# The branch of slot 2 ahead of positions and rounding: a hand-over from attention to experts

## The chip, the cores and the metric

One core of one Trainium2 chip runs the whole program in one launch. The metric is device time in microseconds (us), from the start of the program to its end. The engines are TensorE (PE in the profile; its weight loads are PEld), VectorE (DVE), ScalarE (ACT), GpSimd (POOL) and SyncE (SP, which issues most DMAs). Each engine works through a queue of its own in program order and waits on semaphores of the others.

## The reference

Three layers follow one another on 4608 tokens (batch 8, sequence 576) of 512 features:

```python
k_p, v_p = k.reshape(B, H, 72, 8, D).mean(3), v.reshape(B, H, 72, 8, D).mean(3)   # pooled by 8
attn = softmax(q @ k_p.T / sqrt(64));  x = attn @ v_p            # 8 heads of 64
e_idx = argmax(x @ w_gate);  gate_w = softmax(x @ w_gate)[e_idx]  # 8 experts, one for each token
eom = sigmoid(x @ w_output_gate)
for e in range(8):                                               # w1 (512, 1024), w2 (1024, 512)
    out[e_idx == e] = gate_w * eom[:, e] * (relu(x[e_idx == e] @ w1[e]) @ w2[e])
g = s * relu(out @ w_in) ** 2 + b                                # w_in (512, 2048)
result = g @ w_out                                               # w_out (2048, 512)
```

## The kernel before

Products that need more than the engine's fast format gives are made from a high and a low part: ScalarE writes the high part, another engine subtracts it from the raw value to get the low part (`split`), and TensorE adds three products, high by high, high by low, low by high. So a "cut" of a tile is one ScalarE and one VectorE instruction.

**Attention** goes over 36 tiles of 128 tokens (`NT` = 36), as a pipeline written out by hand: iteration t transposes q of tile t+1 (`s1`), makes the scores of tile t (`s2`: matmuls, then VectorE's maximum L279 and subtraction L282), multiplies the weights of tile t-3 by v (`s4`, L329), transposes the weights of tile t-2 (`s3`, L307), and finishes tile t-4 on VectorE (`s5`, L341 to L357; L357 writes x, which SyncE stores to DRAM at L360). Scores and results have a PSUM tile each (`sc`, `pv`), used in turn. `fill` puts small steps of the router between VectorE's own. At the end of an iteration come its `hooks`: loads of expert 0's weights w1 and w2 and their cutting into eight pieces each (`wt.piece`): ScalarE makes the high part (L1042), another engine the low part (L1044). For w1 the low part is VectorE's, one piece in every second iteration from 20 on; for w2 it is GpSimd's, one in each iteration from 29 on.

**The router** (`Router`) gives each token a place in the list sorted by expert. It counts with matmuls against a triangle (L698 to L705), then writes for each tile a row matrix (`row`, L816), compares tile offsets with slot numbers (`compare`, L856), and inverts the list with 40 small matmuls (`invert`, L864), so that `idx` (L870) holds for each slot of 128 places the tokens to be gathered. It is done in two parts, columns `PRE` to `SOON` (2 to 5) first and the rest later. `tables` (L896 to L923) writes for each slot whether the expert changes (`chg`) and which comes next (`nxt`). `close_ranks` (L926 to L970) corrects the positions for the slots that were done ahead and writes `st`, where each slot's result is stored.

**Slots 0 and 1** belong to expert 0 and are filled from the first 16 tiles, so that TensorE has work while the router finishes (`First`): gather, transpose (`turn`), cut, layer one (L541, 24 matmuls for a slot), relu (L549), transposed h (`turn_h`, L555), its high and low part (`high_h`, `low_h` L565; they lie in the memory of the two slots' x). `Router.finish` runs router steps with this between them.

**`experts`** takes the slots one after another: layer one of slot i (`l1`, L1238 to L1240, 24 matmuls), layer two of slot i-1 (`l2`, L1268, 24 matmuls, PSUM tile `py`, two in turn), transposed h of slot i (`trh`, L1252), transposed x of slot i+2 (`tr`, L1228, PSUM tile `pt`, two in turn). `sw1` and `sw2` are the switches of the weights: ScalarE, VectorE and SyncE load `chg` into a register and branch (L1058, L1059); if the expert changes they cut the loaded weights. `later` holds work that is put behind the next slot's layer one: the cut of x and `result` (L1216, a copy out of PSUM by ScalarE and VectorE, and a store). `side(i, part)` runs a step of `Doubles`, which rounds the last layer's weights from 64-bit words (L1139 to L1156; VectorE, GpSimd and ScalarE in turn), and in slot 3 `token_scale`.

The order ahead of slot 2 is: `l2` of slot 0, `side(0, 0)` with `close_ranks`, `side(0, 1)`, `tr(2)`, `trh` of slot 1, `tr(3)`, `cut_h`, `side(1, 0)`, `side(1, 1)`, `sw1(2)`, layer one of slot 2.

**`Dense`** does the last two layers from about 690 us on.

Of the kernel before, what the change touches and what calls it, by code (L numbers as in the profile page):

```python
# [9 lines left out]
F32 = mybir.dt.float32  # L10
# [39 lines left out]
def attention(ctx, tc, c, q, k, v, wg, wog, xd, lg, ro, wt, room, hooks):  # L50
# [9 lines left out]
    spare = wt.pool.tile([P, 8192], F32, tag="wb", name="kvr")  # L60
    krs = [t[0:KB, 0:kv].rearrange("p (j f) -> p j f", j=NBLK) for t in (spare, wt.raw[1][0])]
    vrs = [spare[:, kv * i:kv * i + kv].rearrange("p (j f) -> p j f", j=NBLK) for i in (1, 2)]
    xbuf = [one.tile([P, DM], F32, name=f"x{i}") for i in range(3)] + [room]
    xbuf = [t.rearrange("p (a h d) -> p a h d", a=2, h=4) for t in xbuf]
    kbd = [one.tile([P, H, 2, SP], F32, name=f"kbd{i}") for i in range(3)]
    vbd = [one.tile([P, NSEG, VW], F32, name=f"vbd{i}") for i in range(3)]
# [271 lines left out]
    def s5(t, pv):  # L338
        pvv = pv[:, :, 0:4 * VW].rearrange("p a (h w) -> p a h w", w=VW)
        rec = p2.tile([P, 2, 4], F32, tag="rec", name="rec")  # L340
        nc.vector.tensor_scalar(out=rec, in0=pvv[:, :, :, VW - 1], scalar1=1e-9, scalar2=None, op0=ALU.add)  # L341
        fill()
        nc.vector.reciprocal(out=rec, in_=rec)
        fill()
        lp = p2.tile([P, 2, 4, G2], F32, tag="lp", name="lp")
        nc.vector.tensor_tensor(
            out=lp, in0=pvv[:, :, :, D:D + G2], in1=rec.unsqueeze(3).to_broadcast([P, 2, 4, G2]), op=ALU.mult
        )
        fill()
        nc.vector.tensor_reduce(  # L350
            out=lg[:, t, :], in_=lp.rearrange("p a h g -> p g (a h)"), axis=AX.X, op=ALU.add
        )
        fill()

        def rest():
            x = xbuf[t % 4]
            nc.vector.tensor_tensor(  # L357
                out=x, in0=pvv[:, :, :, 0:D], in1=rec.unsqueeze(3).to_broadcast([P, 2, 4, D]), op=ALU.mult
            )
            nc.sync.dma_start(out=xd[t * P:(t + 1) * P, :], in_=x.rearrange("p a h d -> p (a h d)"))  # L360

        if t == NT - 1:
            return rest
        rest()
# [58 lines left out]
    for t in range(NT + 4):  # L423
        if t < NT - 5:
            load_q(t + 5)
        if t < NT - 1:
            s1(t + 1)
        rest = s5(*pvs.pop()) if pvs else None
        mask_g()
        if t < NT:  # L430
            s2(t)
        for fn, a in sched.get(t, []):
            fn(*a)
        if t in (NT, NT + 1):
            s3(t - 2)
        if t == 28:
            first.gather(xd)
        if t == NT + 2:
            first.open()
            first.turn(0, ps.tile([P, 512], F32, tag="pe", name="pt0"))  # L440
            first.turn(1, ps.tile([P, 512], F32, tag="pf", name="pt1"))
        if 3 <= t < NT + 3:
            s4(t - 3)
        if 2 <= t < NT:
            s3(t - 2)
        if exps:
            exp_(*exps.pop())
        if t >= NT - 1:
            fill(5)
        while later:  # L450
            later.pop()()
        for a, b in BATCHES:
            if b == t - 3:
                fill(0 if b == NT else 99)
                todo += ro.steps(a, b, lambda: ps.tile([P, 512], F32, tag="prep", name="pr"), later)
        for fn in at_end.get(t, []) + hooks.get(t, []):
            fn()
        if t == NT + 2:
            first.cut(0)
    left, last = todo[:-5], todo[-5:]  # L460
    for f in last:
        f()
        if left:
            left.pop(0)()
    first.layer(0, ps.tile([P, 2, 512], F32, tag="pv", name="ph0"))
    first.run(12)
    first.relu(0)
    first.run(8)
    psv = later.pop()()
    first.run(4)  # L470
    rest()
    first.cut(1)
    for f in left:
        f()

    def between():
        first.relu(1)
        first.layer(1, ps.tile([P, 2, 512], F32, tag="sc", name="ph1"))
        first.run(8)
        first.turn_h(ps.tile([P, 2, 512], F32, tag="pv", name="th0"))  # L480
        first.run(4)
        first.relu(0)

    def behind():
        first.high_h()
        first.run(12)
        first.relu(1)

    inv = [ps.tile([P, NSLOT], F32, tag=n, name="inv") for n in ("pq", "pe")]
    ro.finish(psv, inv, between, behind, first.low_h)  # L490
    return first


class First:
# [35 lines left out]
    def layer(self, i, ph):  # L530
# [2 lines left out]
        wh, wl = [w.rearrange("p (k f) -> p k f", f=FE) for w in self.wt.a]  # L533
        for n in range(2):
            s = slice(n * 512, n * 512 + 512)
            o = ph[:, n]
            for k in range(4):
                for x, w in ((xh, wh), (xh, wl), (xl, wh)):
                    self.todo.append(
# [6 lines left out]
            self.todo.pop(0)()  # L546

    def relu(self, n):
        self.nc.scalar.activation(out=self.hs[self.i][n], in_=self.ph[:, n], func=AF.Relu)  # L549

    def turn_h(self, th):
        self.th = th
# [57 lines left out]
NSLOT = NT + E - 1 + PRE  # L610
ROOM = 5120
WIDE = 4
SOON = 5
MID = N - 2048
BATCHES = [(0, 8), (8, 16), (16, 24), (24, 30), (30, 34), (34, 36)]

# [1 line left out]
class Router:  # L618
# [204 lines left out]
    def finish(self, psv, inv, between, behind, last):  # L823
# [48 lines left out]
            )  # L872


        compare(0, NT, PRE, SOON)
        for step in rows:
            step()
        between()
        invert(inv[0], PRE, SOON)
        for t in range(0, 24, 8):  # L880
            compare(t, t + 8, SOON, NSLOT)
        index(inv[0], PRE, SOON)
        behind()
        compare(24, 32, SOON, NSLOT)
        compare(32, NT, SOON, NSLOT)
        invert(inv[1], SOON, NSLOT)
        last()
        index(inv[1], SOON, NSLOT)
        self.tables()
        V.scalar_tensor_tensor(  # L890
            out=kp["pos"], in0=self.ki, scalar=float(P), in1=self.rf, op0=ALU.mult, op1=ALU.add
# [294 lines left out]
            self.nc.gpsimd.tensor_tensor(out=b[:, o], in0=b[:, x], in1=b[:, y], op=op)  # L1186


def experts(ctx, tc, c, kp, wt, xd, ys, bank, wide, side, ahead, tail, start):
    nc = tc.nc  # L1190
    ident = c["ident"]
    p1 = ctx.enter_context(tc.tile_pool(name="ex1", bufs=1))
# [64 lines left out]
        for n in range(2):  # L1257
            split(nc, hh[n], hl[n], th[n])

    def l2(py, end=False, hh=hh, hl=hl):  # L1260
        wh, wl = [w.rearrange("p (k f) -> p k f", f=DM) for w in wt.b]
        ah, al = [[h[k // 4][:, k % 4 * P:k % 4 * P + P] for k in range(8)] for h in (hh, hl)]
        steps = [[(ah[k], wh[:, k]), (ah[k], wl[:, k]), (al[k], wh[:, k])] for k in range(8)]
# [1 line left out]
            steps = [[s[0] for s in steps], [s[1] for s in steps], [s[2] for s in steps]]  # L1265
        steps = [s for part in steps for s in part]
        for j, (a, w) in enumerate(steps):
            nc.tensor.matmul(py, lhsT=a, rhs=w, start=j == 0, stop=j == len(steps) - 1)  # L1268
        return py

# [21 lines left out]

    gather(2)
    gather(3)
    py = l2(room_y(), True, start.hh, start.hl)
    second(1)
    side(0, 0)
    side(0, 1)
    tr(2)()
    gather(4)  # L1300
    th = trh(start.hs[1])
    wt.raw_new(0)
    second(0)
    later = [tr(3)]
    gather(5)
    cut_h(th)
    later.append(lambda: result(0, py))
    side(1, 0)
    side(1, 1)
    sw1(2)  # L1310
    total = None

    def first(i):
# [7 lines left out]

    def slot(i):
        first(i)
        py = l2(room_y())
        th = trh()
        if i + 2 < NSLOT:
            later.append(tr(i + 2))
        side(i, 0)
        gather(i + 4)
        cut_h(th)  # L1330
# [375 lines left out]
def kernel(  # L1706
# [50 lines left out]
        hooks.setdefault(25 + j, []).append(lambda j=j: wt.load(1, slice(0, 1), part=j))  # L1757
    for j in range(8):
        for what in range(2):
            hooks.setdefault(20 + 2 * j + what, []).append(lambda j=j, w=what: wt.piece(0, j, 8, w))  # L1760
            hooks.setdefault(29 + j + what, []).append(lambda j=j, w=what: wt.piece(1, j, 8, w, nc.gpsimd))
    hooks[29].insert(0, wt.open_b)
    with ExitStack() as x:
        ro = Router(tc, c, lg, kp, wf)
        start = attention(x, tc, c, q, k, v, moe_w_gate, moe_w_output_gate, xd, lg, ro, wt, wf[:, ROOM:ROOM + DM], hooks)
# [13 lines left out]
    def side(i, part):  # L1779
        ahead(i, part)  # L1780
        if part == 0:
            if i == 0:
                close_ranks(tc, c, wide(), kp)
            db.step()
        else:
            if i == 3:
                token_scale(tc, wide(), lg, kp, tok.scale)
            if i % 3 != 2:
                db.step()
            if i > 3:  # L1790
                tok.order(kp["pos"], 1 + (i % 4 == 0))
# [17 lines left out]
    with ExitStack() as x:  # L1809
# [19 lines left out]
            dn.due(8)  # L1829
            db.run(db.end, len(db.pieces))  # L1830

        experts(x, tc, c, kp, wt, xd, ys, bank, wide, side, ahead, tail, start)
    dn.run(ctx)


# [24 lines left out]
```

## Time and profile before

| | |
|---|---|
| median of three runs | 1456.26 us (1454.87 to 1456.47) |
| the profiled execution's own time | 1453.35 us |
| its span, first to last instruction | 1451.5 us |
| TensorE busy | 1405.8 us (97%) |
| VectorE, ScalarE, GpSimd busy | 829.8, 710.3, 438.5 us |
| mean granted TensorE clock | 0.994 of 2.4 GHz |
| chain that ended last: TensorE | 43% of the span |

Busy time is the union of the instructions of an engine; matmuls are pipelined and their ends are modelled. The granted clock is the share of 2.4 GHz that TensorE was given, 0.50 being 1.2 GHz. Idle time is put down to the engine whose semaphore came last.

### The profile page before, as it was taken

The page shows a single profiled execution, that of the slowest core. Times are in us where ns is not written, and L with a number is a line of the kernel's source. Part 1 is how long each engine was busy: PE and PEld are TensorE (multiplying, and loading weights), DVE is VectorE, ACT ScalarE, POOL GpSimd, SP SyncE. Part 2 cuts the span into 40 slices and gives each one's busy share as a digit, 9 for nine tenths or more (in the row PEclk, how much of TensorE's full clock was granted, in tenths as well). Part 3 has the DMA queues.
Part 4 walks back from the last instruction along what each step waited for, and adds up shares of the span by engine and source line. Part 5 has one row for each costly group of instructions (what it writes and reads, how often), then busy time and mean ns, then how long its engine had stood idle before and what let it go on. Part 6 is the DMA issues. An engine that isn't in the chain of part 4 may idle for free.

```text
span 1451.5 us, 22908 instructions
## 1 busy us (share of the span) xinstructions
PE 1405.8 (97%) x7565; PEld 1235.3 (85%) x7565; DVE 829.8 (57%) x1680; ACT 710.3 (49%) x1324; POOL 438.5 (30%) x587
## 2 busy tenths in 40 slices
PE   5999987999999999999999999999999999999998
PEld 5898876888888888888898888898888889888887
DVE  6788874587845668423666544644553464455433
ACT  3666632365634455222656545545555554555443
POOL 4998333454565558307330100010010001001001
PEclk9999998999999999999999999999999999999999
DMA  9996234278775767594765654475465447545441
GB/s 252 298 313 191 95 108 163 88 207 222 209 216 182 217 181 260 151 85 123 244 160 138 181 139 129 118 192 142 116 182 141 126 122 192 139 116 160 118 117 64
DMA packets 203040, 239.43 MB, mean 165 GB/s; under 512 B 66702, under 2 KB 114062, under 8 KB 202894
## 3 DMA queue, kind: packets, MB, share of 16 engines
q1 hardware_dynamic: 195502, 217.22, 54.1%
q0 software_dynamic: 7392, 20.49, 4.9%
q8 instruction: 63, 1.03, 0.3%
q14 instruction: 83, 0.68, 0.2%
HBM read 184.39 MB, written 43.83 MB: 157 GB/s over the span
## 4 chain that ended last, share of the span: by engine, by line
PE 43%; issue 8%; ACT 1%; POOL 0%; DVE 0%; DMA 0%; POOLq 0%; DVEq 0%; ACTq 0%
PE po L1651 8%; PE po L1650 8%; PE po L1649 7%; PE bank L1590 7%; PE bank L1591 7%; PE bank L1592 7%; PE py L1268 0%; POOL out L1661 0%; DMA ring<-ws 0%; ACT wb L1614 0%; ACT y L1613 0%; ACT r L1613 0%; POOLq L1856 0%; ACT yo L1660 0%; ACT hs L1613 0%
## 5 line engine op out<-in xcount | busy, mean ns | idle before, releaser
L1613 ACT ACTIVATE r<-r,s_b 128x384 f32<-128x384 f32 x188 | 133.4, 710 | 275.5 <-DVE r L1606 247.9
L1661 POOL DMA_INDIRECT out<-yo,kp_pos x36 | 35.8, 993 | 662.9 <-ACT yo L1660 537.3
L1268 PE MATMUL py<-wb,hh 128*128 128x512 f32 x608 | 186.3, 389 | 0.3 <-ACT hh L994 0.3
L1605 DVE TENSOR_TENSOR r<-bank,held 128x384 f32<-128x384 f32 x141 | 78.4, 556 | 183.2 <-PE bank L1592 181.7
L1590 PE MATMUL bank<-wa,ring 128*128 128x384 f32 x480 | 162.2, 338 | 1.1 <-ACT xg L1596 0.9
L1591 PE MATMUL bank<-wa,ring 128*128 128x384 f32 x480 | 162.1, 338 | 0.0
L1592 PE MATMUL bank<-wa,ring 128*128 128x384 f32 x480 | 161.0, 335 | 0.0
L1650 PE MATMUL po<-wo,wb 128*128 128x512 f32 x396 | 156.5, 395 | 0.0
L1616 DVE TENSOR_TENSOR wb<-r,wb 128x384 fp32r<-128x384 f32 x188 | 104.7, 557 | 67.7 <-ACT wb L1614 67.7
L1651 PE MATMUL po<-wo,wb 128*128 128x512 f32 x360 | 143.0, 397 | 0.0
L1649 PE MATMUL po<-wo,wb 128*128 128x512 f32 x360 | 140.0, 389 | 0.0
L1268 PEld LDWEIGHTS py<-wb,hh 128*128 128x128 f32 x608 | 114.0, 188 | 24.1 <-ACT hh L994 0.5
L1238 PE MATMUL bank<-wa,xh 128*128 128x512 f32 x296 | 119.7, 404 | 11.6 <-ACTq L1059 11.6
L1141 POOL TENSOR_SCALAR dt<-dt 128x256 f32<-128x256 f32 x64 | 71.4, 1116 | 178.7 <-DVE dt L1140 170.3
L994 ACT ACTIVATE hh<-th 128x512 fp32r<-128x512 f32 x76 | 41.4, 595 | 170.7 <-PE th L1252 170.6
L1268 PE MATMUL py<-wb,hl 128*128 128x512 f32 x304 | 117.4, 390 | 0.0
L1240 PE MATMUL bank<-wa,xl 128*128 128x512 f32 x296 | 116.3, 393 | 0.0
L1239 PE MATMUL bank<-wa,xh 128*128 128x512 f32 x296 | 115.9, 391 | 0.0
L1590 PEld LDWEIGHTS bank<-wa,ring 128*128 128x128 f32 x480 | 90.1, 188 | 16.0 <-ACT r L1602 4.7
L1614 ACT ACTIVATE wb<-r 128x384 fp32r<-128x384 f32 x188 | 98.9, 526 | 6.0
L1591 PEld LDWEIGHTS bank<-wa,ring 128*128 128x128 f32 x480 | 90.1, 188 | 10.4
L995 DVE TENSOR_TENSOR hl<-th,hh 128x512 fp32r<-128x512 f32 x76 | 48.9, 683 | 82.6 <-ACT hh L994 82.6
(305 smaller groups left out, 3195.7 us busy)
## 6 DMA issues: line engine op xcount, KB each, us to landing
ring<-ws SPq DMA_DIRECT2D x336, 256.0 KB
wr<-in_moe_w SPq DMA_DIRECT2D x72, 512.0 KB
ws<-wf SPq DMA_DIRECT2D x16, 896.0 KB
ys<-y SPq DMA_DIRECT2D x37, 256.0 KB
q<-in_q SPq DMA_DIRECT2D x16, 512.0 KB
kvr<-in_v SPq DMA_DIRECT2D x8, 1024.0 KB
dx<-in_moe_w_out SPq DMA_DIRECT2D x32, 256.0 KB
dx<-in_moe_w_in SPq DMA_DIRECT2D x32, 256.0 KB
```

The source lines that it names most:

```text
L1238: nc.tensor.matmul(ph, lhsT=xh[:, k], rhs=wh[:, k, s], start=k == 0, stop=False)
L1239: nc.tensor.matmul(ph, lhsT=xh[:, k], rhs=wl[:, k, s], start=False, stop=False)
L1240: nc.tensor.matmul(ph, lhsT=xl[:, k], rhs=wh[:, k, s], start=False, stop=k == 3)
L1268: nc.tensor.matmul(py, lhsT=a, rhs=w, start=j == 0, stop=j == len(steps) - 1)
L1590: nc.tensor.matmul(o, lhsT=w[:, 0, k], rhs=xh[:, k], start=f, stop=False, skip_group_check=True)
L1591: nc.tensor.matmul(o, lhsT=w[:, 0, k], rhs=xl[:, k], start=False, stop=False, skip_group_check=True)
L1592: nc.tensor.matmul(o, lhsT=w[:, 1, k], rhs=xh[:, k], start=False, stop=False, skip_group_check=True)
L1613: lambda: nc.scalar.activation(out=r, in_=r, func=AF.Identity, scale=s_b[:, 0:1], bias=s_b[:, 1:2]),
L1616: [lambda: nc.vector.tensor_tensor(out=gl, in0=r, in1=gh.bitcast(F32), op=ALU.subtract)],
L1649: nc.tensor.matmul(o, lhsT=gh[:, s], rhs=wh, start=first, stop=False)
L1650: nc.tensor.matmul(o, lhsT=gh[:, s], rhs=wl, start=False, stop=False)
L1651: nc.tensor.matmul(o, lhsT=gl[:, s], rhs=wh, start=False, stop=last)
```

## The change

- In `experts`, `tr(2)` is issued in the middle of slot 0's second layer (after 12 of its 24 matmuls), and `sw1(2)` stands right behind the loads of the next weights. `close_ranks` and the router's second part (inversion and index of the later slots, now `others`, with a PSUM tile of `pt`) come in slot 2, behind its layer one. The four rounding steps of slots 0 and 1 go; slots 2, 5, 8 and 11 have one more each. The result of slot 0 (`y0`) is queued in slot 2, so that it runs in slot 3.
- `SOON` is 6 instead of 5: the first part of the index serves the gathers up to slot 5.
- In `Router.finish` the first index comes before slot 1's first layer has gone on, `low_h` before the last two compares.
- w2's low parts are made on VectorE. w1's pieces are cut one in each iteration from 19 on, w2's from 28 on.
- x has a fifth buffer for tiles below 24, in the memory of k and v.
- Slot 0's x is transposed and cut one iteration earlier, slot 1's one step earlier; the PSUM tiles that `First` uses are others.

```diff
-    xbuf = [one.tile([P, DM], F32, name=f"x{i}") for i in range(3)] + [room]
+    xbuf = [...] + [room, spare[:, 3 * kv:3 * kv + DM]]
-            x = xbuf[t % 4]
+            x = xbuf[t % (5 if t < 24 else 4)]
...
-        if t == NT + 2:
+        if t == NT + 1:
             first.open()
-            first.turn(0, ps.tile([P, 512], F32, tag="pe", name="pt0"))
-            first.turn(1, ps.tile([P, 512], F32, tag="pf", name="pt1"))
+            first.turn(0, ps.tile([P, 512], F32, tag="pq", name="pt0"))
+        elif t == NT + 2:
+            first.turn(1, ps.tile([P, 512], F32, tag="pe", name="pt1"))
...
-        if t == NT + 2:
-            first.cut(0)
+        if t in (NT + 1, NT + 2):
+            first.cut(t - NT - 1)
...
-    first.layer(0, ps.tile([P, 2, 512], F32, tag="pv", name="ph0"))
-    first.run(12)
-    first.relu(0)
+    wide = ps.tile([P, 2, 512], F32, tag="pv", name="ph0")
+    first.layer(0, [wide[:, 0], wide[:, 1]])
+    first.run(16)
+    psv = later.pop()()
     first.run(8)
-    psv = later.pop()()
-    first.run(4)
     rest()
-    first.cut(1)
...
     def between():
+        first.relu(0)
         first.relu(1)
-        first.layer(1, ps.tile([P, 2, 512], F32, tag="sc", name="ph1"))
-        first.run(8)
+        first.layer(1, [ps.tile([P, 512], F32, tag=n, name="ph1") for n in ("pq", "pf")])
+        first.run(5)
+
+    def behind():
+        first.run(6)
         first.turn_h(ps.tile([P, 2, 512], F32, tag="pv", name="th0"))
-        first.run(4)
+        first.high_h()
+        first.run(1)
         first.relu(0)
-
-    def behind():
-        first.high_h()
         first.run(12)
         first.relu(1)
...
-SOON = 5
+SOON = 6
...
+        def others(ps):
+            invert(ps, SOON, NSLOT)
+            index(ps, SOON, NSLOT)
...
         between()
-        invert(inv[0], PRE, SOON)
+        invert(inv, PRE, SOON)
+        index(inv, PRE, SOON)
+        behind()
         for t in range(0, 24, 8):
             compare(t, t + 8, SOON, NSLOT)
-        index(inv[0], PRE, SOON)
-        behind()
+        last()
         compare(24, 32, SOON, NSLOT)
         compare(32, NT, SOON, NSLOT)
-        invert(inv[1], SOON, NSLOT)
-        last()
-        index(inv[1], SOON, NSLOT)
...
-    py = l2(room_y(), True, start.hh, start.hl)
+    y0 = l2(room_y(), True, start.hh, start.hl, lambda: tr(2)())
+    gather(4)
     second(1)
-    side(0, 0)
-    side(0, 1)
-    tr(2)()
-    gather(4)
     th = trh(start.hs[1])
     wt.raw_new(0)
     second(0)
+    sw1(2)
+    cut_h(th)
     later = [tr(3)]
     gather(5)
-    cut_h(th)
-    later.append(lambda: result(0, py))
-    side(1, 0)
-    side(1, 1)
-    sw1(2)
...
     def slot(i):
         first(i)
+        if i == PRE:
+            close_up()
+            others(ps.tile([P, DM], F32, tag="pt", name="inv")[:, 0:NSLOT])
         py = l2(room_y())
         th = trh()
         if i + 2 < NSLOT:
             later.append(tr(i + 2))
+        if i == PRE:
+            later.append(lambda: result(0, y0))
...
-            hooks.setdefault(20 + 2 * j + what, []).append(lambda j=j, w=what: wt.piece(0, j, 8, w))
-            hooks.setdefault(29 + j + what, []).append(lambda j=j, w=what: wt.piece(1, j, 8, w, nc.gpsimd))
-    hooks[29].insert(0, wt.open_b)
+            for i, t in ((0, 19), (1, 28)):
+                hooks.setdefault(t + j + what, []).append(lambda i=i, j=j, w=what: wt.piece(i, j, 8, w))
+    hooks[28].insert(len(hooks[28]) - 1, wt.open_b)
...
-            if i == 0:
-                close_ranks(tc, c, wide(), kp)
             db.step()
...
-            if i % 3 != 2:
+            if i % 3 != 2 or i < 14:
                 db.step()
```

## Rows read from the trace of the kernel before

**Rows 1.** Busy table by stretch: engine's busy us (instructions), clock, DMA share, GB/s.
```profile
core 0: us, PE busy (x) PEld busy (x) DVE busy (x) ACT busy (x) POOL busy (x), PEclk, DMA share, GB/s
...
190.40:213.90 23.50, 20.95 (x173) 16.56 (x173) 17.78 (x72) 4.67 (x10) 4.50 (x5) 1.00 0.28 91
213.90:227.20 13.30, 1.73 (x17) 1.49 (x15) 10.00 (x33) 3.04 (x7) 7.68 (x8) 0.73 1.01 350
227.20:234.30 7.10, 7.10 (x25) 5.56 (x26) 0.18 (x1) 2.31 (x5) 0.93 (x2) 0.78 0.40 160
234.30:640.00 405.70, 405.70 (x1990) 340.44 (x1989) 248.44 (x413) 181.24 (x304) 206.42 (x231) 1.00 0.67 180
```

**Rows 2.** Timeline of TensorE, hand-over: start, length, instruction, count, [idle before, releaser].
```profile
203.73 2.97 PE L541 MATMUL ph<-wa,first 128*128 128x512 f32 x12
...
208.12 5.73 PE L1268 MATMUL py<-wb,first 128*128 128x512 f32 x24 [0.41 <-DVE kp_idx L870]
213.69 0.60 PE L1228 MATMUL pt<-ident,xg 128*128 128x128 f32 x4
...
227.17 0.80 PE L1238 MATMUL bank<-wa,xh 128*128 128x512 f32 x1 [11.57 <-ACTq L1059]
```

**Rows 3.** Timelines of VectorE and ScalarE ahead of the branch.
```profile
207.89 0.51 DVE L900 TENSOR_TENSOR wf<-kp_tend,iota_s 1x360 f32<-1x360 f32 x1
...
211.86 0.15 DVE L934 COPY dy<-kp_cnt 128x8 f32<-128x8 f32 x1
...
218.17 0.19 DVE L970 TENSOR_REDUCE kp_st<-dy 1x1 int32<-1x45 f32 x1
...
226.97 0.41 DVE L995 TENSOR_TENSOR wo<-dt,wo 128x256 fp32r<-128x256 f32 x1
...
226.38 0.42 ACT L994 ACTIVATE wo<-dt 128x256 fp32r<-128x256 f32 x1 [3.72 <-POOL dt L1156]
```

**Rows 4.** Timelines in attention: GpSimd's L1044, VectorE and TensorE.
```profile
160.11 2.49 POOL L1044 TENSOR_TENSOR wb<-wr,wb 128x512 fp32r<-128x512 f32 x2
...
160.44 2.71 DVE L1044 TENSOR_TENSOR wa<-wr,wa 128x512 fp32r<-128x512 f32 x1
...
164.94 3.38 PE L329 MATMUL pv<-vbd,eT 128*128 128x162 f32 x12 [2.06 <-DVE vbd L208]
...
170.60 1.94 PE L329 MATMUL pv<-vbd,eT 128*128 128x162 f32 x12
...
186.15 3.73 POOL L1044 TENSOR_TENSOR wb<-wr,wb 128x512 fp32r<-128x512 f32 x3
...
186.89 3.03 DVE L671 TENSOR_TENSOR wf<-lg,wf 128x32 f32<-128x32 f32 x1
```

**Rows 5.** Timelines: the low part of slot 0's h, and the gather of slot 2.
```profile
206.57 1.29 DVE L565 TENSOR_TENSOR first<-th,first 128x512 fp32r<-128x512 f32 x2 [1.88 <-PE ph L541]
...
204.81 1.06 POOL L1219 DMA_INDIRECT xg<-xd,kp_idx  x1 [3.32 <-DVE wf L856]
```

**Rows 6.** Timelines of slots 2 and 3: VectorE behind layer one, TensorE's layer one.
```profile
234.49 0.69 DVE L1244 TENSOR_SCALAR hs<-bank 128x512 f32<-128x512 f32 x1 [7.11 <-PE bank L1240]
...
235.92 0.69 DVE L1216 COPY y<-py 128x512 uint16<-128x512 uint16 x1
...
240.97 0.48 PE L1238 MATMUL bank<-wa,xh 128*128 128x512 f32 x1
...
246.54 0.62 PE L1268 MATMUL py<-wb,hh 128*128 128x512 f32 x2
```

**Rows 7.** A stop without a fall of the clock, and a slice after a fall.
```profile
30.68 0.28 PE L163 MATMUL prl<-ident,kp 72*128 72x72 f32 x1 [1.92 <-ACT kbd L158]
...
166.00:167.00 1.00, 1.00 (x6) 1.00 (x5) 0.37 (x1) 0.00 (x0) 0.00 (x0) 0.50 0.30 113
```

**Rows 8.** Timeline of VectorE, iteration 22 of attention.
```profile
119.71 0.17 DVE L341 TENSOR_SCALAR rec<-pv 128x8 f32<-128x8 f32 x1 [0.63 <-PE pv L329]
```

**Rows 9.** Timelines of GpSimd and VectorE while the router writes rows.
```profile
194.08 1.61 POOL L816 TENSOR_SCALAR wf<-iota_r,wf,num 128x128 f16<-128x128 bf16 x2 [4.21 <-DVE wf L807]
...
194.72 0.17 DVE L671 TENSOR_TENSOR wf<-lg,wf 128x16 f32<-128x16 f32 x1
```

More of the change, by code (lines that the diff above doesn't have):

```diff
@@ L62, in attention @@
     vrs = [spare[:, kv * i:kv * i + kv].rearrange("p (j f) -> p j f", j=NBLK) for i in (1, 2)]
-    xbuf = [one.tile([P, DM], F32, name=f"x{i}") for i in range(3)] + [room]
+    xbuf = [one.tile([P, DM], F32, name=f"x{i}") for i in range(3)] + [room, spare[:, 3 * kv:3 * kv + DM]]
     xbuf = [t.rearrange("p (a h d) -> p a h d", a=2, h=4) for t in xbuf]
@@ L476, in between @@
     def between():
+        first.relu(0)
         first.relu(1)
-        first.layer(1, ps.tile([P, 2, 512], F32, tag="sc", name="ph1"))
-        first.run(8)
+        first.layer(1, [ps.tile([P, 512], F32, tag=n, name="ph1") for n in ("pq", "pf")])
+        first.run(5)
+    def behind():
+        first.run(6)
         first.turn_h(ps.tile([P, 2, 512], F32, tag="pv", name="th0"))
-        first.run(4)
+        first.high_h()
+        first.run(1)
         first.relu(0)
-    def behind():
-        first.high_h()
         first.run(12)
         first.relu(1)
-    inv = [ps.tile([P, NSLOT], F32, tag=n, name="inv") for n in ("pq", "pe")]
-    ro.finish(psv, inv, between, behind, first.low_h)
+    ro.finish(psv, ps.tile([P, NSLOT], F32, tag="pe", name="inv"), between, behind, first.low_h)
     return first
@@ L535, in layer @@
             s = slice(n * 512, n * 512 + 512)
-            o = ph[:, n]
+            o = ph[n]
             for k in range(4):
@@ L548, in relu @@
     def relu(self, n):
-        self.nc.scalar.activation(out=self.hs[self.i][n], in_=self.ph[:, n], func=AF.Relu)
+        self.nc.scalar.activation(out=self.hs[self.i][n], in_=self.ph[n], func=AF.Relu)
     def turn_h(self, th):
@@ L1186, in sums, with experts @@
             self.nc.gpsimd.tensor_tensor(out=b[:, o], in0=b[:, x], in1=b[:, y], op=op)
-def experts(ctx, tc, c, kp, wt, xd, ys, bank, wide, side, ahead, tail, start):
+def experts(ctx, tc, c, kp, wt, xd, ys, bank, wide, side, ahead, tail, start, others, close_up):
     nc = tc.nc
@@ L1258, in cut_h, with l2 @@
             split(nc, hh[n], hl[n], th[n])
-    def l2(py, end=False, hh=hh, hl=hl):
+    def l2(py, end=False, hh=hh, hl=hl, mid=None):
         wh, wl = [w.rearrange("p (k f) -> p k f", f=DM) for w in wt.b]
@@ L1267, in l2 @@
         for j, (a, w) in enumerate(steps):
+            if mid and j == 12:
+                mid()
             nc.tensor.matmul(py, lhsT=a, rhs=w, start=j == 0, stop=j == len(steps) - 1)
@@ L1830, in tail @@
             db.run(db.end, len(db.pieces))
-        experts(x, tc, c, kp, wt, xd, ys, bank, wide, side, ahead, tail, start)
+        experts(x, tc, c, kp, wt, xd, ys, bank, wide, side, ahead, tail, start, ro.others,
+                lambda: close_ranks(tc, c, wide(), kp))
     dn.run(ctx)
```

1 line of the change is left out of this document (added).

## The prediction

> **What bounds the kernel now.** I read the busy table in stretches first. From 234.3 us to 640 us TensorE is busy for 405.7 of 405.7 us, so nothing that VectorE, ScalarE or GpSimd do there sets the time as long as it stays hidden; what can be won is idle TensorE before that, and a lower clock. The hand-over from attention to the experts has most of it: 2.55 us idle in 190.4 to 213.9, 11.57 us idle in 213.9 to 227.2, and then 7.1 us at a mean granted clock of 0.78 [rows 1]. The timeline of TensorE shows the one long hole: after the transposes of slot 3 it waits 11.57 us for ScalarE's queue at the branch L1059, which is the switch of w1 ahead of slot 2 (`sw1(2)`) [rows 2]. No weight changes there; the first matmul of slot 2 only has to know that the branch has been passed. What stands ahead of the branch is seen on the other engines [rows 3]: VectorE makes the tables and `pos` (14 instructions, 207.89 to 211.86), then `close_ranks` (24, to 218.36), then four rounding steps, which go back and forth between VectorE, GpSimd and ScalarE; ScalarE's last one is at 226.38 and VectorE's at 226.97. So ScalarE and VectorE are the bound there, not by their load but by the order of their queues.
>
> The second place is inside attention [rows 4]. GpSimd's tensor_tensor at L1044 (w2's low parts) and VectorE's instructions with two SBUF inputs keep each other out: VectorE's L1044 takes 2.71 us at 160.44 and its small L671 takes 3.03 us at 186.89, each while GpSimd runs a train of L1044. After the first one TensorE stands for 2.06 us at 164.94, and its next twelve matmuls take 3.38 us, against 1.94 us for the same twelve at 170.60.
>
> **The change, part by part.** All sums are made in the profiled execution: span 1451.5, its own time 1453.35 us, 2.91 us under the median of 1456.26. I carry differences over to the median.
>
> *The branch and what stood before it.* `close_ranks` and the four rounding steps leave the queue ahead of `sw1(2)`. I follow the new order from 190.4 us on. Layer one of slot 0 no longer waits for its low part (cut one iteration earlier). The count of the last batch still meets its one-hot at about 194.5; ranks, offsets, the compare (four columns instead of three) and the last rows end at about 198.1, where TensorE, having 16 + 8 + 5 matmuls to do meanwhile, has waited some 0.4 us. The first inversion follows, then the other 19 matmuls of slot 1's layer one with the eight transposes, which end at about 204.5 (before: at 206.7 [rows 2]). Then comes a wait that the change makes: `low_h` overwrites the x of slot 1, so it can't begin before that layer has ended; it takes 1.29 us [rows 5], and it is now VectorE's last reader of attention's PSUM. In the trace of before the second layer of slot 0 started at 208.12 just behind VectorE's L870 [rows 2], which was then the last reader, though its data were there earlier; so the second layer waits for `low_h`: 1.35 us, start at about 205.9. I charge 2.0 us of idle for this stretch (0.4, 1.35 and small change) instead of 14.12: **12.1 us won**. The second inversion of 40 matmuls moves into slot 2 and is neither won nor lost.
>
> Does the branch then come in time? VectorE: `low_h` to 205.85, two compares (0.7), tables and `pos` (3.97 [rows 3]) to 210.5, the low part of slot 2's x (0.68) to 211.2, branch at about 211.5. TensorE needs 24 matmuls, two transposed x and one transposed h, and is ready at about 213.4. Slack 1.9 us. Does the x of slot 2 come in time for a transpose in mid layer? Its gather was issued at 204.81 and read at 213.69 without a wait, 8.9 us later [rows 2, 5]; now it is issued behind the earlier index at about 200.1 and read at 208.7, 8.6 us later. At worst that is 0.3 us.
>
> *The clock.* With no hole of 11.57 us the first layer of slot 2 runs at full clock: 7.1 us in before [rows 1], 5.57 us for slot 3's layer one, 240.97 to 246.54 [rows 6]: **1.5 us won**.
>
> *Slot 3 pays.* The result of slot 0 (`y0`) was copied out of PSUM in slot 2; now the copy is queued in slot 3, behind layer one. Slot 3's second layer takes the same PSUM buffer (two in turn), so it waits for VectorE's copy, behind which nothing can hide: VectorE first makes h (L1244, which needs the end of layer one), the low x, the branch, then the copy. In slot 2 of before that row runs from 234.49 to 235.92 + 0.69 = 236.61, while TensorE went on at once [rows 6]. **2.2 us lost**. Whether the clock falls after such a stop is open: a stop of 2.06 us was followed by slices at 0.50 (that is 1.2 GHz) and cost about 1.7 us, one of 1.92 us at 30.68 was not [rows 4, 7]. Bounds 0 and 1.7; 2.2 us is nearest to the stop that was followed by a fall, but the two rows lie only 0.14 us apart, so I take half: **0.85 us lost**.
>
> *Low parts of w2 on VectorE.* Eight more instructions of 0.68 us there, 5.4 us; since w1's parts go from every second iteration to every one, eight even iterations (20 to 26, 30 to 36) get one more. Where VectorE has a hole the part fits: in iteration 22 it idles 0.63 us at 119.71 [rows 8]. I charge 0.6 us for iterations without one and 0.5 us for ScalarE's high parts, which come ahead of the masked v. Against this the two trains of GpSimd's L1044 go. The first cost 2.06 us of wait and 1.7 us of low clock [rows 4]: 3.8 us. The second's effect lies in the 2.55 us above and isn't counted twice. Sum: **2.6 us won**; bounds from -2 (all eight parts and the high parts show in full: 4.8 + 1.0 - 3.8) to 3.8.
>
> By the Trainium skill (SBUF — State Buffer, section "Who interferes with whom") a VectorE instruction with two SBUF inputs contends with any GpSimd instruction that reads SBUF, whoever comes first holding the pair for its whole instruction. By that rule the moved parts would also be held by GpSimd's trains of L816; the rows bear it out for L1044 and not for L816 [rows 4, 9]; by the rule alone the sum below would be 3 us, as in the fourth rival.
>
> *At nothing.* The fifth x buffer (the list of waits has no VectorE wait for a store of x), transposing slot 0's x one iteration earlier (same work), the order of SyncE's loads, and rounding steps in slots 5, 8 and 11 instead of ahead of slot 2 (about 1.4 us of VectorE each, under a TensorE that never waits there [rows 1]; uncovered they would cost 4.2 us). `close_ranks` and the second index lie on VectorE in slot 2 (6.7 us) and end some 2 us before slot 3's layer one does.
>
> Sum: 12.1 + 1.5 - 2.2 - 0.85 + 2.6 = 13.15 us. The profiled execution would be 1440.2, the median 1443.1.
>
> **The rivals.**
> *Slot 3 doesn't pay* (20%): the copy is out of the way in time or the next buffer free. Against it: L1244 can't precede the end of layer one. Gain 16.2, 1440.1 us.
> *VectorE sets attention's pace* (15%): holes like that of [rows 8] are few, and every moved part shows. Gain 13.15 - 4.6 = 8.5, 1447.7 us.
> *The branch still comes late* (9%): VectorE's queue of `low_h`, compares, tables, low x is 1.9 us ahead by my chain; if the moved work upstream delays it by 7 us, 5 us of the hole stay. Gain 8.1, 1448.1 us.
> *GpSimd's L816 holds the parts* (4%): the router gives GpSimd trains of eight and six of 0.8 us each [rows 9]; a part queued near their start would wait some 5 us each time, 10 us in all; gain 3.1, 1453.1 us. Against it: at 194.72 L671, with two SBUF inputs, takes 0.17 us in the midst of two L816 [rows 9].
> *Slower* (3%): GpSimd's rounding keeps VectorE out in slots 2 and 3 as its L1044 did in attention. In slot 2 VectorE has 10.4 us of work (`close_ranks` and index 6.7, four operations of 512 columns 2.6, a rounding step 1.1) for some 13 us, so 3 us more are hidden; from there each us shows. If half of it took four times as long, as L1044 did [rows 4], 10.4 would become 26: 13 us late, and a quarter of that again in slot 3: 13.1 - 16.3, 1459.4 us. Against it: GpSimd has one step there at a time.
>
> **How the numbers follow.** The forecast has 49%: **1443 us**. From 0.2% (2.9 us) on a measurement of this kernel can tell a change. It and the first three rivals are faster, 93%; the case of L816 is about the same, 4%; 3% slower. The range takes in the two rivals at 1440 and 1448 with 2 us for the unknown clock on either side: 1438 to 1450.
>
> **What would show it.** Right: the first matmul of slot 2 within 2 us of the last transpose, at about 211 us instead of 227; the granted clock at 1.0 there; a stop of 1 to 1.5 us ahead of slot 0's second layer behind `low_h`; one of about 2.2 us ahead of slot 3's second layer behind VectorE's L1216; no VectorE L1044 over 1 us. Wrong: a hole of more than 3 us at L1238, iterations of attention longer than before on the whole, or VectorE's L1216 not in that place.

## The result and the profile after

The changed kernel takes 1441.99 us (median of 5 runs, 1438.0 to 1447.84) against 1456.26 us (5 runs, 1454.87 to 1456.69): ratio 0.9905, 95% interval 0.9877 to 0.9932. In a second set of five runs it took 1438.63 us against 1455.06: 0.9889 (0.9872 to 0.9905). So 14.3 and 16.4 us are won, where 13.15 were forecast. The execution whose profile is read here is the slowest, 1447.84 us with a span of 1445.9; what makes it slow lies in attention, most of it early.

The busy table by stretch, the hand-over to answer [rows 1]: busy us (instructions) of PE, PEld, DVE, ACT and POOL, granted clock, DMA share, GB/s.

```profile
core 0: us, PE busy (x) PEld busy (x) DVE busy (x) ACT busy (x) POOL busy (x), PEclk, DMA share, GB/s
195.50:217.60 22.10, 20.78 (x146) 16.97 (x146) 14.44 (x57) 4.54 (x10) 5.78 (x6) 1.00 0.31 98
217.60:223.20 5.60, 5.60 (x27) 4.47 (x25) 1.29 (x2) 2.09 (x5) 0.95 (x1) 1.00 1.00 331
223.20:236.80 13.60, 13.56 (x101) 11.20 (x100) 9.84 (x34) 4.08 (x9) 4.00 (x4) 1.00 0.64 249
236.80:640.00 403.20, 401.02 (x1959) 336.26 (x1960) 249.78 (x420) 181.49 (x306) 208.76 (x234) 1.00 0.66 184
```

Up to slot 2's first matmul TensorE is idle for 1.32 us, where it was 14.12 [rows 1], and slot 2's layer one takes 5.6 us at full clock instead of 7.1. The stretch of before begins 1.1 us ahead of layer one and holds a wait of 1.01 us there; from layer one on it is 1.32 against 13.1. Timeline of TensorE, the kernel before:

```profile
191.38 0.18 PE L698 MATMUL pr<-oh,tri 128*128 128x32 bf16 x1 [1.01 <-DVE oh L682]
```

The timeline of TensorE (start, length, instruction, count, [idle before, releaser]) shows the two stops that are left in the changed kernel, to be held against [rows 2]:

```profile
210.41 2.98 PE L1273 MATMUL py<-wb,first 128*128 128x512 f32 x12 [1.32 <-DVE first L565]
213.23 0.60 PE L1231 MATMUL pt<-ident,xg 128*128 128x128 f32 x4
...
217.31 0.60 PE L1231 MATMUL pt<-ident,xg 128*128 128x128 f32 x4
217.67 0.47 PE L1241 MATMUL bank<-wa,xh 128*128 128x512 f32 x1
...
223.22 1.18 PE L864 MATMUL inv<-wf 128*128 128x39 f16 x40
...
238.98 0.74 PE L1273 MATMUL py<-wb,hh 128*128 128x512 f32 x2 [2.22 <-DVE y L1219]
```

The first matmul of slot 2 (L1241, L1238 before) follows the last transposes (L1231) with no wait; it starts at 217.67 here, where attention ran late, and at 208.97 in w1_slow (below), where it did not. The second layers (L1273) have 1.32 us ahead of slot 0's, behind `low_h`, and 2.22 us ahead of the one in slot 3, behind VectorE's copy. VectorE's timeline shows both writers, and what stands ahead of the branch now (against [rows 3, 5, 6]):

```profile
208.98 1.29 DVE L565 TENSOR_TENSOR first<-th,first 128x512 fp32r<-128x512 f32 x2 [3.81 <-PE ph L541]
...
214.67 0.18 DVE L893 SCALAR_TENSOR_TENSOR kp_pos<-wf 128x36 int32<-128x36 int32 x1
214.78 0.67 DVE L998 TENSOR_TENSOR xl<-pt,xh 128x512 fp32r<-128x512 f32 x1
...
236.80 0.69 DVE L1247 TENSOR_SCALAR hs<-bank 128x512 f32<-128x512 f32 x1 [2.49 <-PE bank L1243]
237.41 0.68 DVE L998 TENSOR_TENSOR xl<-pt,xh 128x512 fp32r<-128x512 f32 x1
238.23 1.29 DVE L1219 COPY y<-py 128x512 uint16<-128x512 uint16 x2
```

VectorE's last work ahead of the branch ends at 215.45, 2.2 us before slot 2's first matmul. The prediction had 211.2 and 213.4 for these two, 2.2 us as well, and 1.9 from the branch itself, whose time these rows don't show.

What the forecast did not contain is in the changed kernel's timeline of TensorE in attention:

```profile
58.93 0.31 PE L199 MATMUL pf<-wgt,vt 128*128 128x32 f32 x2
63.43 1.09 PE L253 MATMUL pq<-ident,q 128*128 128x128 f32 x4 [4.19 <-DMA q<-in_q]
64.31 2.13 PE L273 MATMUL sc<-kbd,qT 128*128 128x144 f32 x8
```

The busy table there:

```profile
60.00:64.00 4.00, 0.57 (x3) 0.60 (x4) 0.41 (x2) 0.41 (x1) 3.69 (x8) 0.87 1.08 370
64.00:68.00 4.00, 4.00 (x23) 3.94 (x22) 1.49 (x2) 1.07 (x3) 3.61 (x8) 0.70 1.02 334
```

A load of q comes 4.19 us late, the clock falls behind it, and iteration 10 (an iteration t is counted from the scores' maximum L279 of tile t-1 to that of tile t) takes 10.0 us instead of 4.25.

To see where time goes in every run, I cut each profiled execution at three instants of its timeline: the first L541 (end of attention), slot 2's first matmul, and the dense layers' first matmul; the last stage runs to the end of the span. A stage is the difference of two starts in that table of instructions:

| us | attention | to slot 2 | slots | dense |
|---|---|---|---|---|
| before | 191.51 | 35.66 | 461.16 | 763.17 |
| after | 195.55 | 22.12 | 464.92 | 763.31 |
| c_after (same kernel) | 191.01 | 22.14 | 464.86 | 763.19 |
| undo_handover | 187.21 | 33.90 | 466.62 | 763.17 |
| tables_first | 187.51 | 23.20 | 470.16 | 763.33 |
| round_first | 187.55 | 26.43 | 466.91 | 763.51 |
| gp_low | 193.63 | 22.12 | 463.23 | 763.32 |
| old_parts | 191.81 | 22.31 | 463.21 | 763.17 |
| w1_slow | 186.84 | 22.13 | 463.26 | 763.17 |
| four_x | 187.43 | 22.13 | 463.27 | 763.17 |
| y0_early | 193.56 | 22.15 | 460.70 | 763.19 |
| y0_early_2 | 190.57 | 22.12 | 460.72 | 763.19 |
| w1_slow_y0 | 190.29 | 22.13 | 460.73 | 763.45 |
| all_three | 187.31 | 21.53 | 462.02 | 763.24 |

The middle stages repeat to a few hundredths; attention does not. With one and the same program for attention (after, c_after, undo_handover, tables_first, round_first, both y0_early) it took 187.2 to 195.6 us.

### The profile page after: what moved, and what is told of

The parts are those of the page before. It is cut to its first block, busy times and chain, and to the rows that moved or that the text cites. A ratio compares the mean times of both kernels' runs of the same rounds, so it can differ in the third digit from the quotient of the medians.

```text
span 1445.9 us, 22912 instructions
## 1 busy us (share of the span) xinstructions
PE 1404.5 (97%) x7565; PEld 1234.1 (85%) x7565; DVE 830.3 (57%) x1688; ACT 711.5 (49%) x1324; POOL 428.2 (30%) x579
## 4 chain that ended last, share of the span: by engine, by line
PE 44%; issue 8%; ACT 1%; POOL 0%; DVE 0%; DMA 0%; POOLq 0%; DVEq 0%; ACTq 0%
PE po L1655 8%; PE po L1654 8%; PE po L1653 7%; PE bank L1594 7%; PE bank L1595 7%; PE bank L1596 7%; PE py L1273 0%; POOL out L1665 0%; DMA ring<-ws 0%; ACT wb L1618 0%; ACT y L1617 0%; ACT r L1617 0%; POOLq L1859 0%; ACT yo L1664 0%; ACT hs L1617 0%
## 5 line engine op out<-in xcount | busy, mean ns | idle before, releaser
L1273 PE MATMUL py<-wb,hh 128*128 128x512 f32 x608 | 187.8, 392 | 2.5 <-DVE y L1219 2.2
L1273 PEld LDWEIGHTS py<-wb,hh 128*128 128x128 f32 x608 | 114.5, 189 | 27.0 <-DVE y L1219 2.6
L1241 PE MATMUL bank<-wa,xh 128*128 128x512 f32 x296 | 119.1, 402 | 0.0
L1273 PE MATMUL py<-wb,hl 128*128 128x512 f32 x304 | 117.9, 392 | 0.0
L1242 PE MATMUL bank<-wa,xh 128*128 128x512 f32 x296 | 115.2, 389 | 0.0
```

Of the source, the lines that this page charges most:

```text
L1241: nc.tensor.matmul(ph, lhsT=xh[:, k], rhs=wh[:, k, s], start=k == 0, stop=False)
L1242: nc.tensor.matmul(ph, lhsT=xh[:, k], rhs=wl[:, k, s], start=False, stop=False)
```

## The experiments

**The changed kernel again**, as the control.

> The changed kernel again, as the control of these runs. If the late load of q in iteration 10 (PE stood 4.19 us at L253, and the clock fell to 0.70 there) is a chance event of single executions, the times spread again over 1438 to 1448 us, and the profiled execution may be without that wait at about 1442 us; if it belongs to the new kernel, the wait is there again and the median stays at 1442 to 1446.

Measured: 1438.63 us (1437.36 to 1442.94), and no wait on q. So that wait doesn't come in every execution. Another disturbance came instead; the busy table of 40 to 44 us in the control:

```profile
40.00:44.00 4.00, 4.00 (x21) 3.83 (x21) 2.42 (x7) 1.58 (x6) 3.61 (x8) 0.62 0.80 234
```

The same stretch of undo_handover, whose program for attention is the same:

```profile
40.00:44.00 4.00, 4.00 (x34) 3.94 (x33) 2.70 (x10) 2.69 (x9) 3.61 (x8) 1.00 0.90 288
```

At a mean granted clock of 0.62 TensorE does 21 instructions where it does 34 at 1.00, and iteration 6 takes 6.30 instead of 4.65 us.

**The hand-over undone, whole and by halves.** undo_handover puts all of this ahead of `sw1(2)` again; tables_first only `close_up` and `others`, round_first only the rounding steps `side`, with `cut_h` ahead of `sw1(2)` too (in both kernels with `side` the extra steps of slots 5, 8 and 11 go). What is put here goes out of slot 2.

```diff
     second(0)
+    side(0, 0)
+    side(0, 1)
+    close_up()
+    others(ps.tile([P, DM], F32, tag="pt", name="inv")[:, 0:NSLOT])
+    cut_h(th)
+    side(1, 0)
+    side(1, 1)
     sw1(2)
-    cut_h(th)
...
```

> The changed kernel with one part undone: the four rounding steps of the dense weights, the ranks and the late slots' index stand ahead of slot 2's branch again, as before. Theory (the prediction's): the branch's tests wait for that work on VectorE and ScalarE, so the first matmul of slot 2 is late again by 10 to 13 us behind the last transposes, and the time rises by 10 to 14 us to 1452 to 1457. Rival (the time was won in attention and at its end, and slot 2's wait only moved there): less than 4 us slower, under 1447.

> The changed kernel with only the ranks and the late slots' index put back ahead of slot 2's branch; the four rounding steps stay behind it. Theory (the branch's tests on VectorE wait for all that is queued ahead; the ranks and the index hold VectorE for about 6.5 us): first matmul of slot 2 is 4 to 7 us late, 4 to 8 us slower with the clock. Rival (the index's matmuls on PE and the ranks alone are covered by slot 0's second layer, the rounding was the whole of the wait): under 1.5 us.

> The changed kernel with only the four rounding steps put back ahead of slot 2's branch; the ranks and the index stay behind it. Theory: the rounding is what the branch stands behind on ScalarE (the wait of before was L1059's on ScalarE), 6 to 10 us late and 7 to 11 us slower. Rival (it is VectorE's tables that set the end, as those left ahead of the branch end only 2 us before it): 2 to 4 us.

Measured: 1453.28 us for the whole, ratio to before 0.9988 (0.9979 to 0.9998), so 14.7 us over the control and nearly all of the gain gone (attention keeps its 4.3 us, but the stage of the slots, with slot 3's stop and the low clock, takes 5.5 us more than before); 1446.72 us, 0.9936 (0.9916 to 0.9957), for the tables; 1448.61 us, 0.9943 (0.9924 to 0.9961), for the rounding. TensorE's timeline at slot 2, undo_handover:

```profile
221.11 0.79 PE L1241 MATMUL bank<-wa,xh 128*128 128x512 f32 x1 [10.46 <-ACTq L1062]
```

The same of tables_first:

```profile
214.58 0.79 PE L1242 MATMUL bank<-wa,xh 128*128 128x512 f32 x1 [3.40 <-DVEq L1062]
```

And of round_first:

```profile
213.98 0.50 PE L1241 MATMUL bank<-wa,xh 128*128 128x512 f32 x1 [4.06 <-ACTq L1062]
```

The hole returns with the old releaser, ScalarE's queue at the branch, and the halves differ in the way one should learn to see: the first matmul (L1241) reads the weight's high part, which ScalarE may cut, and waits for ScalarE's branch; the second (L1242) reads the low part and waits for VectorE's. By stages (to slot 2 plus slots) the whole costs 13.5 us against c_after, the tables 6.4 and the rounding 6.3: each alone is about half, and together they nearly add up. These are single executions, all four with a fall of the clock behind slot 3's stop; the medians put the halves 8.1 and 10.0 us over the control. Each is a stop of 3.4 or 4.1 us and a stretch of low clock behind it.

**Slot 0's result copied one slot earlier**, with only its store left in slot 3:

```diff
-    later = [tr(3)]
+    later = [tr(3), lambda: y0c.append(copied(y0))]
...
-            later.append(lambda: result(0, y0))
+            later.append(lambda: result(0, None, y=y0c[0]))
```

> The changed kernel with the copy of slot 0's result out of PSUM moved from slot 3 into slot 2, behind the transposes of slot 3's x; only its store stays in slot 3. Theory (slot 3's second layer waits for VectorE's copy): the stop of 2.2 us ahead of L1273 and the clock of 0.83 behind it go, 2 to 4 us are won, 1438 to 1440 if the control is at 1442. Rival (the stop only absorbs time that PE would lose in the next slots anyway, or the copy now delays slot 2's own relu): within 1 us of the control.

> The early copy of slot 0's result alone, a second time. Theory (it wins 2.5 to 4.2 us behind slot 2, and its first four runs met attention at its slower times by chance): where attention takes its 187 us, the span is 187.2 + 22.1 + 460.7 + 763.2 = 1433.2, the time 1435; at least one run in five is there, and the median is 1435 to 1438. Rival (what it wins is taken back elsewhere in each execution): all runs are again between 1438 and 1442 us.

Measured: 1439.04 us (1438.69 to 1441.62), the control's time, and the second time 1435.66 us (1434.74 to 1438.62), ratio 0.9861 (0.9844 to 0.9877). By the total of the first four runs I should have put the edit at nothing. The stages say otherwise: 460.7 us behind slot 2 in both executions, against 463.2 or 464.9. Timelines of VectorE and TensorE in the second set's profiled execution:

```profile
219.88 0.69 DVE L1219 COPY y<-py 128x512 uint16<-128x512 uint16 x1
...
231.62 0.62 PE L1273 MATMUL py<-wb,hh 128*128 128x512 f32 x2
```

The copy lies a slot ahead of its user and L1273 has no idle time before it. The profiled execution of the first set met attention at 193.56; of the other three only the time is known, and it fits an attention near 191. Three of the second's four spans are 1432.8 to 1433.8, the 1433.2 of the sum. It wins 2.5 us where the clock stays up behind the stop, 4.2 where it falls.

Whether it falls differs between executions. The ten us around the same stop of 2.22 us in c_after, busy table:

```profile
230.00:240.00 10.00, 7.78 (x27) 5.89 (x27) 3.85 (x8) 2.41 (x6) 3.38 (x4) 0.83 0.33 106
```

And in gp_low:

```profile
230.00:240.00 10.00, 7.78 (x35) 6.08 (x34) 6.00 (x13) 2.95 (x7) 5.68 (x6) 1.00 0.26 82
```

The slots took 464.86 us in the one and 463.23 in the other: such a fall costs 1.6 us.

**Whose low parts, and when.** Three kernels vary the weights' pieces: w2's low parts on GpSimd again (gp_low), w1's pieces in every second iteration again (w1_slow), and both as before (old_parts).

```diff
-            for i, t in ((0, 19), (1, 28)):
...
+            for i, t, eng in ((0, 19, None), (1, 28, nc.gpsimd)):      # gp_low
...
+            for i, t in ((0, 20 + j), (1, 28)):                        # w1_slow
...
+            hooks.setdefault(20 + 2 * j + what, [])...                 # old_parts: w1
+            hooks.setdefault(29 + j + what, [])...                     # old_parts: w2, on nc.gpsimd
```

> The changed kernel with the low parts of w2 formed on GpSimd again (in the same iterations as the change has them). Theory (GpSimd's two-input parts keep VectorE out): iterations 32 and 33 cost near 5.9 us again instead of 4.24 and 3.94, and layer one of slot 0 starts 3 to 4 us later than in an undisturbed execution of the control (186 to 187 us); about 3.5 us slower. Rival (those iterations got shorter by the other edits, the earlier transposes and the spread-out pieces): within 1.5 us of the control.

> The changed kernel with the pieces of w1 formed in every second iteration from 20 on, as before, and those of w2 on VectorE in every iteration from 28 on. Theory (one piece of w1 an iteration, beside the router's rows, makes VectorE set the pace in iterations 23 to 26, which cost 3.2 to 3.7 us against the kernel before): those iterations run as before and 1 to 4 us are won, unless the two weights' pieces now meet in iterations 28 to 35. Rival (they meet: up to two VectorE parts of 0.69 us in an iteration): the loss moves to iterations 28 to 35 and the time is within 1.5 us of the control or over it.

> The changed kernel with the weights' pieces as before: w1's every second iteration from 20 on, w2's low parts on GpSimd from 29 on. Theory after the run with GpSimd's low parts alone (it kept iterations 32 and 33 at 3.9 us: what hurts is not GpSimd's part by itself but one that meets a part of VectorE's, and w1's were done by then): now they meet again, one VectorE part takes near 2.7 us as before, and iterations 32 and 33 cost together 3 to 4 us more; 1441 to 1443 us in executions with attention undisturbed. Rival (those 3.7 us came with the earlier transposes or the fifth x buffer): iterations 32 and 33 stay at 3.9 to 4.4 us, and the time within 1.5 us of 1438.

Measured: gp_low 1438.23 us (0.9878, 0.9859 to 0.9897), w1_slow 1439.53 (0.9897, 0.9882 to 0.9912), old_parts 1442.41 (0.9917, 0.9904 to 0.9930). The first is a miss of mine: GpSimd's parts cost nothing by themselves, iterations 32 and 33 took 3.94 and 3.95 us with them. Only old_parts brings the loss back, 5.83 and 5.97 us (its median alone, whose interval touches the control's, would not show it). Timelines of its GpSimd, VectorE and TensorE, beside [rows 4]:

```profile
160.43 2.49 POOL L1047 TENSOR_TENSOR wb<-wr,wb 128x512 fp32r<-128x512 f32 x2
...
160.79 2.69 DVE L1047 TENSOR_TENSOR wa<-wr,wa 128x512 fp32r<-128x512 f32 x1
...
165.26 3.25 PE L329 MATMUL pv<-vbd,eT 128*128 128x162 f32 x12 [2.03 <-DVE vbd L208]
```

It is the meeting of a w1 part on VectorE with two w2 parts on GpSimd: VectorE's part begins 0.36 us behind GpSimd's first and ends 0.56 us behind the end of the second. In gp_low w1's parts are over by iteration 27, so the engine that makes w2's no longer matters. Starts of the scores' maximum (L279) in iterations 31 to 33, VectorE's timeline of the kernel before:

```profile
158.98 0.76 DVE L279 TENSOR_REDUCE mx<-sc 128x8 f32<-128x576 f32 x1 [0.29 <-PE sc L273]
...
164.83 0.75 DVE L279 TENSOR_REDUCE mx<-sc 128x8 f32<-128x576 f32 x1
...
170.81 0.76 DVE L279 TENSOR_REDUCE mx<-sc 128x8 f32<-128x576 f32 x1 [0.60 <-PE sc L273]
```

And of undo_handover, which has the change's attention:

```profile
159.31 0.76 DVE L279 TENSOR_REDUCE mx<-sc 128x8 f32<-128x576 f32 x1
...
163.54 0.76 DVE L279 TENSOR_REDUCE mx<-sc 128x8 f32<-128x576 f32 x1 [0.29 <-PE sc L273]
...
167.48 0.76 DVE L279 TENSOR_REDUCE mx<-sc 128x8 f32<-128x576 f32 x1
```

11.83 us become 8.17: 3.66 won. w1_slow spreads w1's parts over 20 to 35 again, with w2's on VectorE too: iterations 32 and 33 take 4.43 and 4.31 there, and up to iteration 25 it gains 1.4 us on undo_handover, so the sum (186.84 against 187.21) and the time hardly move. The 1.4 us have a reason that can be read in the busy table of iterations 24 to 26, undo_handover first, then w1_slow:

```profile
122.22:136.51 14.29, 13.09 (x142) 12.23 (x142) 14.16 (x43) 9.28 (x24) 13.15 (x23) 1.00 0.49 148
121.53:135.07 13.54, 12.85 (x142) 12.20 (x142) 12.85 (x42) 9.09 (x24) 12.33 (x23) 1.00 0.53 161
```

With a part of w1 in every iteration VectorE is busy for 14.16 of 14.29 us there, so it sets the pace. These three iterations take 13.9 to 17.7 us in the nine executions with a part in every iteration, most in those that were late by then, and 13.5 to 13.7 in the five with one in every second, late or not.

**Four buffers for x** instead of five (`xbuf[t % 4]`).

> The changed kernel with four buffers for attention's rows instead of five up to iteration 23. Theory (the fifth lets VectorE's x go ahead of the stores, and PE's wait on x at L329, 1.2 us twice before, is what it saves): 1 to 2 us slower. Rival (the stores are no bound; the fifth buffer is worth nothing, or its stores are what makes q late in iteration 10): within 1 us of the control, and no wait on q at L253.

Measured: 1443.64 us (1438.12 to 1446.74), 0.9925 (0.9910 to 0.9940). That is 5 us over the control, whose interval ends at 0.9905, but 1.7 over the first set of the changed kernel (1441.99, 0.9877 to 0.9932), and its six times lie within the ten of five buffers (1437.36 to 1447.84). The profiled execution is the fastest of the six and its stages are those of five buffers. So what the fifth buffer is worth is not shown. The theory's wait on x ahead of L329 doesn't go with it: at 39.56 in the changed kernel it is 1.19 us, in before it was 1.18 at 39.65. The profiled execution has no late q, but neither has the control's, so whether the fifth buffer's stores make q late stays open.

**Edits together.** w1_slow_y0 joins w1_slow and y0_early; all_three also gives slot 0's low half (`hl`) memory of its own, in w2's raw tile, so that `low_h` need not wait for slot 1's layer one.

> Two edits of before together: the early copy of slot 0's result and w1's pieces every second iteration. By stages of the first runs (attention up to layer one 186.8, from there to slot 2's first matmul 22.1, from there to the dense layers 460.7 instead of 464.9, then 763.2) the span is 1432.8 and the time 1434.6 us, 4 us under the control, if attention runs undisturbed. Rival (the early copy is paid back in attention, where the four runs of it alone all came out 4 us over the sum): 1437 to 1440 again.

> The changed kernel with three edits: the early copy of slot 0's result, w1's pieces every second iteration, and the low half of slot 0's layer one in other memory, so that VectorE need not wait for slot 1's layer one to write it. Theory: the stop of 1.3 us ahead of slot 0's second layer goes and the stage from layer one to slot 2 takes 20.8 instead of 22.1 us; with the sums of the last run, 1435 us with attention at 190.3, 1433 with it at 187. Rival (that stop is set by slot 1's layer one and its relu, which release attention's PSUM, and not by the low half): the stop stays within 0.5 us under another name, 1436 to 1438.

Measured: 1437.78 us (1437.23 to 1438.60), 0.9869 (0.9852 to 0.9887), and 1436.27 us (1434.92 to 1438.97), 0.9878 (0.9864 to 0.9893). In all_three the stop ahead of slot 0's second layer changes its name, as the rival said, but is halved, by TensorE's timeline:

```profile
201.54 3.02 PE L1275 MATMUL py<-wb,first 128*128 128x512 f32 x12 [0.69 <-ACT first L551]
```

ScalarE's relu of slot 1's layer one is next. The 0.6 us are not seen in the total: the next stage takes 1.3 us more than with the early copy alone (462.02 against 460.72), and 0.65 of that is a wait of the dense layers' first matmul for its weights:

```profile
670.86 0.41 PE L1602 MATMUL bank<-wa,ring 128*128 128x384 f32 x1 [0.65 <-DMA ring<-ws]
```

The two fastest medians are the second one of y0_early and that of all_three, the two lowest ratios to before those of y0_early's second set and of w1_slow_y0; all their intervals touch the control's, so the faster version is shown by the stage (2.5 to 4.2 us behind slot 2, in three executions) and not by its total.

## Why the prediction was right, step by step

- **The hand-over: 12.1 us won.** Measured 12.8 (14.12 to 1.32 us idle), of which 11.8 lie behind the start of layer one. The chain held: VectorE 2.2 us early, second layer behind `low_h` with 1.32 us against 1.35. The 0.4 us for the ranks were not needed. That it is the cause was tested by undo_handover; that the prediction named the order of both queues, not their load, by the two halves.
- **Clock in slot 2: 1.5 won.** Measured 1.5 (7.1 to 5.6 us).
- **Slot 3 pays 2.2, and 0.85 for the clock.** Measured 2.22, and 1.6 in two of six executions that have the stop with no other disturbance behind slot 2 (after and c_after against gp_low, old_parts, w1_slow and four_x). The forecast's half of 1.7 was a fair price for a fall that comes or stays away. y0_early shows what the first rival would have been worth, 2.5 to 4.2 us.
- **Low parts of w2: 2.6 won, the mis-sized term.** In an undisturbed execution attention is 4.3 us shorter (191.51 to 187.21). Of this 1.0 us is the second train of GpSimd's parts, TensorE's wait of 1.01 us at 191.38. It lies in the 14.12 us of [rows 1] and so in the 12.8 above; the prediction was right not to count it twice. (From iteration 35 to layer one before took 12.77 us, old_parts 12.76, with the same wait, gp_low 11.71 and the changed kernel 11.70.) The other 3.2 are this term: the 3.8 us for the first meeting measured 3.66, and the 1.1 us that I charged for more work on VectorE measured 0.4 (iteration 35 starts 3.23 us earlier). The reason given was half wrong: not the engine counts but that VectorE's w1 parts and GpSimd's w2 parts no longer meet. And the 0.4 holds for undisturbed executions alone; in those that were late, iterations 24 to 26 took up to 4 us more than with a part in every second iteration. So the rival in which VectorE sets attention's pace came true in part.
- **The sum.** With the terms as measured 15.3 us are won without a fall of the clock in slot 3 and 13.7 with it; the stages, with attention at 187.21, give 15.7 and 14.1. The medians, 14.3 and 16.4 us apart, hold executions with late attention as well, for which the sum had no term: that the number came this close is in part luck.
- **No VectorE L1044 over 1 us**: one was, 1.13 us at 129.79 in the profiled execution, beside GpSimd's pooling of k.
- **The fifth buffer at nothing**: neither shown nor refuted; the medians without it and with it differ by 1.7 or 5 us, by which set of the changed kernel is taken, and no trace here shows a reason.
- **Attention's iterations not longer**: wrong for the profiled execution, whose attention took 4.0 us more than before, by events that the forecast had no term for: q late in iteration 10 (here 4.19 us, in gp_low 2.05 us), or a fall of the clock near 42 us; and iterations 24 to 26, 17.26 us where undo_handover needs 14.29, which goes with w1's part in every iteration and so with the change. This is why the runs spread over 10 us. What makes q late, and whether the change makes it likelier, stays open.

The rule of the Trainium skill that the prediction weighed (SBUF — State Buffer, section "Who interferes with whom") lets a VectorE instruction with two SBUF inputs contend with any GpSimd instruction that reads SBUF. For GpSimd's L1047, with two inputs, the traces agree (2.69 us above). For L816 it is GpSimd that pays; timelines of GpSimd and VectorE in the changed kernel, and of GpSimd in gp_low, where no part of VectorE meets the train:

```profile
186.20 5.22 POOL L816 TENSOR_SCALAR wf<-iota_r,wf,num 128x128 f16<-128x128 bf16 x6 [17.30 <-DVE wf L807]
...
188.50 0.69 DVE L1047 TENSOR_TENSOR wb<-wr,wb 128x512 fp32r<-128x512 f32 x1 [0.16 <-ACT wb L1045]
...
184.34 4.66 POOL L816 TENSOR_SCALAR wf<-iota_r,wf,num 128x128 f16<-128x128 bf16 x6 [4.82 <-DVE wf L807]
```

In the midst of six of GpSimd's tensor_scalars VectorE's part takes its usual 0.69 us. GpSimd's six take 0.56 us more than alone: one takes 1.17 us and one 0.96, both beside a part of VectorE, the others 0.79. So there is contention here too, but it doesn't hold VectorE, and the fourth rival had no ground.

## What to carry to other kernels

When an engine's branch ends a wait, list everything queued ahead of it on each engine that takes the branch: each engine's branch guards other operands, and moving half of the list left about half of the loss. Price a stop with and without a fall of the clock behind it, for the same stop did both here. And when totals of one kernel spread by 5 to 10 us (two sets of five of this one differ by 3.4 us in the median, more than the 2.9 that the prediction held to be enough), cut the profiled executions into stages: an edit worth 2.5 to 4 us was invisible in a median of four and repeated to 0.02 us in its stage.

## What the runs showed of the hardware

- A stop of TensorE of 2.22 us was followed by a mean granted clock of 0.83 over ten us in some executions and 1.00 in others, with the same instructions around it; the difference was worth 1.6 us.
- Which of VectorE and GpSimd is held up depends on GpSimd's instruction: next to two of its two-input tensor_tensors of 128x512 a VectorE part took 2.69 us, until both had ended; amid its tensor_scalars of 128x128 the part took 0.69 us, and two of the tensor_scalars beside its parts 1.17 and 0.96 us instead of 0.79. Whether it is the inputs, the width or the type that makes the difference, no run separates.
- Attention, with the same program, took 187.2 to 195.6 us in seven profiled executions; the falls of the clock (0.62 at 40 to 44 us) and late loads come and go, and part of such a loss is regained by later iterations (round_first lost 1.7 us in iteration 6 and was level with undo_handover in iteration 25).
